# A retention layer and two feed-forward networks on one core: new start address of the right-hand pools, new pacing of the second network's weight preparation

## The chip, the core and the metric

The kernel runs on one NeuronCore of a Trainium2 chip. Times are device microseconds of one execution of the whole program on that core, from its first to its last instruction and the little that lies around them; lower is better. The core's engines have a queue of instructions each: TensorE (PE, with its weight loads as PEld), VectorE (DVE), ScalarE (ACT), GpSimd (POOL) and SyncE (SP), which here issues all data transfers (DMA).

## What is computed

```python
scores = (q @ k.T) / sqrt(64);  ret = scores * Dmat[head]      # retention: Dmat = gamma**(i-j), i >= j
x = (ret @ v)                        # 4 x 8 heads, 576 positions, 64 wide -> x: 2304 x 512
h = x @ w_in                         # first network: 512 -> 2048
x = (max(h, 0) + alpha * min(h, 0)) @ w_out               # 2048 -> 512
y = (sigmoid(x @ w_gate) * (x @ w_val)) @ w_out2          # second network: 512 -> 1536 -> 512
```

Inputs and output are float32 except the weights, which come as float64.

## The kernel before, in words

The 2304 tokens are cut into five blocks of 256, 512, 512, 512 and 512 (blocks 0 to 4). A float32 operand is held as two halves, hi and lo, both of TensorE's fast float32 type, and a product is three matmuls: hi·hi, hi·lo, lo·hi (`products`, L562). The 128x128 operand is loaded as weights, the operand of 512 (in block 0: 256) columns streams past it; the text calls it the moving operand. ScalarE makes hi by a copy and VectorE makes lo by a subtraction (`split`, L183).

**First network.** `ffn1_h(j, f)` (L573) computes one 128-row slice f of h for block j in 12 matmuls into a PSUM tile `h` (two buffers), ScalarE makes max(h,0) and max(-h,0) (L580, L581), VectorE joins them (L582), and `split` makes the pair `g` (L185, L186). `ffn1_y(j, f)` (L604) multiplies g into four accumulators in 12 matmuls. In blocks 2 to 4, h of slice f is followed on TensorE by y of f-2, h of f+1, y of f-1 and h of f+2. The last of these takes the PSUM buffer of h of slice f and can start only when VectorE's split of slice f has read it. Blocks 0 and 1 run woven together, since the weights are still being converted there; between the slices of blocks 1 to 3 lie the pieces of the retention for the next block. The moving operand of h is the tile `x`, that of y is `g`.

**Second network.** For the block pairs (1, 2) and (3, 4) the gate and value products use a 2x2 scheme of seven products instead of eight (`z_step`, L667, six steps t per pair), then `o_phase` multiplies by the output weights. Block 0 is done plainly at the end (`plain_z`). The seven-product scheme needs weight combinations (`prepare_quarters`, L251), which are made during the first network, stored in DRAM (`td`) and fetched again as `tq`. It also needs combinations of the x blocks (`left_factors`, L639: four adds on GpSimd and seven splits), made for the first pair during block 4.

**One job** of `prepare_quarters` takes two raw weight tiles (512 KB each). For each raw tile ScalarE runs two instructions (L208, L209) and VectorE three (L212, L213, L216), which turn float64 into float32; then GpSimd makes four subtractions (L267), and four times ScalarE copies (L276) and VectorE subtracts (L277); five or so transfers write the result. There are twelve such jobs. The generator of a job is advanced by one stage at each `second_step()` (L320), and `second_pace(every)` (L334), called once per slice f from block 2 on, begins a new job at each `every`-th call.

**Who sets the order.** TensorE's instructions stand in the order of the program. Those of the other four engines are placed by a scheduler, which may move an instruction far ahead of where the program has it. `behind("act", "dve")` (L176) holds it back: everything issued inside is placed after the third most recent urgent split (the splits of g, x and the second network's middle tiles). Before the change it is used in `advance()`, for the first network's weights.

**Memory.** SBUF tiles of 4,096 bytes per partition (slots) come from the left side, where each begins 256 bytes past a multiple of 4,096. Three pools begin at the right end instead: `pad`, `xp` (two tiles of 16 KB, the x blocks) and, after the first network, `wide` (eight slots in their place, seven of which hold `tq` of the odd steps t).

Of the kernel before, what the change touches and what calls it, by code (L numbers as in the profile page):

```python
# [10 lines left out]
F32 = mybir.dt.float32  # L11
# [8 lines left out]
P = 128  # L20
# [36 lines left out]
PACE_B, PACE_C = 0.34, 0.5  # L57


PACE_T = (5, 3)  # L60


def chunks():
# [39 lines left out]
def retention_two_ffn(ctx: ExitStack, tc: tile.TileContext, att, cst, alpha, w1, w2, out):  # L103
# [11 lines left out]


    pad = ctx.enter_context(tc.tile_pool(name="pad", bufs=1, side="right"))
    pad_sb = pad.tile([P, 8], F32, tag="pad", name="pad_sb")
    nc.gpsimd.memset(pad_sb, 0.0)
    x_only = ctx.enter_context(ExitStack())  # L120
    xp = x_only.enter_context(tc.tile_pool(name="xp", bufs=2, side="right"))
# [54 lines left out]
    def behind(*engines):  # L176
        stack = ExitStack()
        for e in engines:
            if len(urgent[e]) > AHEAD:
                stack.enter_context(tc.issue_after(urgent[e][-1 - AHEAD].ins))  # L180
        return stack
# [137 lines left out]

    def second_step():  # L320
        for job, g in list(second):
            if next(g, StopIteration) is StopIteration:
                second.remove((job, g))
                ready.add(job)

    def need(*job):
        while job not in ready:
            if not second or asked:
                begin_job()
            second_step()  # L330
# [3 lines left out]
    def second_pace(every):  # L334
        second_step()
        due[0] += 1
        if due[0] >= every:
            due[0] = 0
            begin_job()
        elif due[0] >= every - 2:  # L340
            ask()
# [456 lines left out]
    def plain_z(f, ws):  # L798
        nb = BLOCKS[0]
        ps = []  # L800
        for w, (pool, tag) in zip(ws, ((ps_h, "h"), (ps_a, "ab"[f % 2]))):
            ps.append(pool.tile([P, nb], F32, tag=tag, name=f"z0_{f}"))
            products(ps[-1], [(w[:, k // 2, k % 2], x0[k // 2][:, :, k % 2]) for k in range(KC)])
            free(w)
        t = small.tile([P, nb], F32, tag="t", name=f"sg0_{f}", bufs=1)
        nc.scalar.activation(t, ps[0], AF.Sigmoid)
        nc.vector.tensor_tensor(out=ps[1], in0=t, in1=ps[1], op=ALU.mult)
        g = half_of_slot(f"p0_{f}")
        split(g[:, 0], g[:, 1], ps[1])
        return g  # L810
# [10 lines left out]
    done = [0]  # L821
# [40 lines left out]
    for j in range(1, NBLK):  # L862
# [13 lines left out]
        for f in range(first, NF1):  # L876
# [4 lines left out]
            if j > 1:  # L881
                second_pace(PACE_T[j == NBLK - 1])
            if j == NBLK - 1:
# [22 lines left out]
    def in_z(n, t):  # L906
        def between(point):
            if point == 0:
                while late:
                    ffn1_y(*late.pop(0))  # L910
            if point == 1 and t + 1 < NSTEP:
                load_quarters(t + 1)
            begin_job() if point % 2 else None
            second_step()
        return between
# [31 lines left out]
    for f in range(NF2):  # L947
# [3 lines left out]
        g = plain_z(f, ws.pop(f))  # L951
# [51 lines left out]
```

## Time and profile before

| what | value |
|---|---|
| median of 3 runs (lowest, highest) | 929.73 us (926.93, 930.13) |
| the profiled execution, its own time | 931.73 us |
| its span, first to last instruction | 930.0 us |
| mean granted TensorE clock, share of 2.4 GHz | 0.991 |
| busy: TensorE, its weight loads | 893.7 us, 742.7 us |
| busy: VectorE, ScalarE, GpSimd | 470.1, 406.2, 118.0 us |
| moved to and from HBM | 171.83 MB read, 47.19 MB written |

How to read it: a busy share is the time in which at least one instruction of an engine ran. Matmuls overlap, so that the start of one group to the start of the next tells their rate better than their durations do. "Idle before" a group is time in which the engine had nothing running, and the name behind the arrow is what ended it.

The stages of the span: 0 to 43 us the first retention pieces, 43 to 160 us blocks 0 and 1 woven, 160 to 203 us the rest of block 1, 203 to 302 us block 2, 302 to 413 us block 3, 413 to 508 us block 4, then the second network: 508 to 701 us blocks 1 and 2, 701 to 874 us blocks 3 and 4, 874 to 930 us block 0.

### The profile page before, as it was taken

Reading aid. Unit: us, or ns where it says so; the run is one execution under the profiler, and the core shown is the slowest. Engines: PE = TensorE matmul, PEld = TensorE weight load, DVE = VectorE, ACT = ScalarE, POOL = GpSimd, SP = SyncE. Lnnn points to the kernel's source line nnn. Section 1 sums busy time; section 2 is a strip of 40 time slices with the busy share of each in tenths; the row PEclk is TensorE's granted clock in tenths of the full one; section 3 lists DMA queues with packets and bytes.
Section 4 is the critical chain, followed back from the end, with each engine's and each line's share of the span. In section 5 each row is a group of like instructions: output and inputs, shape, how many; then the busy total and the mean of one; then the engine's idle time right before and its main releaser. Section 6 shows DMA issues by size and latency. Waiting matters only on the chain.

```text
span 930.0 us, 13173 instructions
## 1 busy us (share of the span) xinstructions
PE 893.7 (96%) x4890; PEld 742.7 (80%) x4890; DVE 470.1 (51%) x765; ACT 406.2 (44%) x772; POOL 118.0 (13%) x111
## 2 busy tenths in 40 slices
PE   5689899999999999999989999999999999999998
PEld 5578788778888878888778888888888888888897
DVE  2799996434444656376954464566333332422121
ACT  3488884333343644367645354444323222422111
POOL 5100004221110231032710010002010000000000
PEclk9799999999999999999999999999999999999999
DMA  9435786733366574479597989899746552469940
GB/s 293 167 115 176 259 310 206 281 137 113 125 214 225 193 262 140 173 255 376 214 384 265 373 347 369 310 340 350 274 147 235 186 192 68 164 247 348 405 194 23
DMA packets 74063, 219.89 MB, mean 236 GB/s; under 512 B 12048, under 2 KB 13072, under 8 KB 74000
## 3 DMA queue, kind: packets, MB, share of 16 engines
q1 hardware_dynamic: 74000, 219.05, 65.7%
q8 instruction: 39, 0.64, 0.3%
q14 instruction: 24, 0.20, 0.1%
HBM read 171.83 MB, written 47.19 MB: 236 GB/s over the span
## 4 chain that ended last, share of the span: by engine, by line
PE 68%; DMA 10%; DVE 10%; ACT 5%; issue 3%; SPq 2%; POOL 2%; ACTq 0%; DVEq 0%; POOLq 0%
PE a L566 14%; PE h L566 10%; PE y L566 10%; PE o_y L566 7%; DMA r<-w 5%; PE z L566 4%; PE c L566 4%; PE b L566 4%; PE e L566 4%; PE o_h L566 4%; DVE r L213 2%; PE o L566 2%; PE o_b L566 2%; PE o_a L566 2%; DVE r L216 1%
## 5 line engine op out<-in xcount | busy, mean ns | idle before, releaser
L566 PE MATMUL h<-x,w 128*128 128x512 f32 (+1 forms) x684 | 151.3, 370 | 14.1 <-DVE g L186 12.1
L566 PEld LDWEIGHTS h<-x,w 128*128 128x128 f32 x684 | 115.6, 190 | 40.2 <-DVE g L186 15.1
L566 PE MATMUL a<-xf,tq 128*128 128x512 f32 x576 | 137.7, 391 | 0.0
L566 PEld LDWEIGHTS a<-xf,tq 128*128 128x128 f32 x576 | 108.2, 188 | 23.3
L566 PE MATMUL y<-g,w 128*128 128x512 f32 x492 | 120.7, 394 | 0.0
L566 PEld LDWEIGHTS y<-g,w 128*128 128x128 f32 x492 | 92.3, 189 | 21.6 <-issue 0.9
L582 DVE SCALAR_TENSOR_TENSOR h<-h,na_sb,t 128x512 f32<-128x512 f32 (+1 forms) x80 | 56.1, 702 | 85.0 <-ACT h L581 84.8
L580 ACT ACTIVATE t<-h 128x512 f32<-128x512 f32 (+1 forms) x80 | 44.1, 551 | 81.1 <-PE h L566 80.9
L566 PE MATMUL o_y<-wo,pp 128*128 128x512 f32 x288 | 73.2, 389 | 0.0
L208 ACT ACTIVATE r<-r 128x512 f32<-128x512 f32 x68 | 45.9, 675 | 53.0 <-DMA r<-w 52.7
L566 PE MATMUL h<-x,v 128*128 128x512 f32 x276 | 68.8, 397 | 0.0
L566 PE MATMUL y<-g,v 128*128 128x512 f32 x276 | 67.0, 392 | 0.0
L566 PEld LDWEIGHTS o_y<-wo,pp 128*128 128x128 f32 x288 | 54.1, 188 | 11.3
L186 DVE TENSOR_TENSOR pp<-p,pp 128x512 fp32r<-128x512 f32 x48 | 34.9, 734 | 54.5 <-ACT pp L185 53.4
L185 ACT ACTIVATE g<-h 128x512 fp32r<-128x512 f32 (+1 forms) x80 | 44.2, 552 | 40.7 <-DVE h L582 40.4
L186 DVE TENSOR_TENSOR g<-h,g 128x512 fp32r<-128x512 f32 (+1 forms) x80 | 50.7, 634 | 22.0 <-ACT g L185 18.5
L566 PEld LDWEIGHTS h<-x,v 128*128 128x128 f32 x276 | 51.1, 187 | 12.5 <-issue 0.2
L566 PEld LDWEIGHTS y<-g,v 128*128 128x128 f32 x276 | 51.5, 188 | 11.8 <-issue 0.5
L267 POOL TENSOR_TENSOR r<-r,r 128x256 f32<-128x256 f32 x24 | 24.7, 1027 | 284.7 <-DVE r L216 284.7
L185 ACT ACTIVATE pp<-p 128x512 fp32r<-128x512 f32 x48 | 30.0, 630 | 60.5 <-PE o_h L566 32.2
L213 DVE CUSTOM_DVE_ANT_0 r<-r,top 128x1024 uint16<-128x1024 uint16 x68 | 48.1, 712 | 3.6 <-ACT r L209 1.0
L216 DVE SCALAR_TENSOR_TENSOR r<-r 128x512 uint32<-128x512 uint32 x68 | 47.3, 699 | 0.5
(102 smaller groups left out, 1293.2 us busy)
## 6 DMA issues: line engine op xcount, KB each, us to landing
tq<-td SPq DMA_DIRECT2D x84, 512.0 KB, 5.0
r<-w SPq DMA_DIRECT2D x68, 512.0 KB, 5.2
wo<-wod SPq DMA_DIRECT2D x60, 512.0 KB, 5.8
v<-w1d SPq DMA_DIRECT2D x46, 512.0 KB, 5.0
td<-q SPq DMA_DIRECT2D x36, 512.0 KB, 4.5
zp<-td SPq DMA_DIRECT2D x48, 256.0 KB, 5.7
kv<-att SPq DMA_DIRECT2D x16, 512.0 KB, 4.5
qk<-att SPq DMA_DIRECT2D x15, 512.0 KB, 4.7
```

What stands on the lines that cost most here:

```text
L185: a = nc.scalar.activation(hi, src, AF.Copy)
L186: d = nc.vector.tensor_tensor(out=lo, in0=src, in1=hi.bitcast(F32), op=ALU.subtract)
L208: nc.scalar.activation(high.bitcast(F32), high.bitcast(F32), AF.Copy, scale=2.0 ** -112)
L213: nc.vector.tensor_tensor(out=low.bitcast(I32), in0=low.bitcast(I32), in1=top.bitcast(I32), op=ALU.add)
L216: nc.vector.scalar_tensor_tensor(low, high, 0x80000000, low, ALU.bitwise_and, ALU.bitwise_or)
L267: sub = lambda o, a, b: nc.gpsimd.tensor_tensor(out=o, in0=a, in1=b, op=ALU.subtract)
L566: nc.tensor.matmul(ps, l, r, start=first and i == 0, stop=last and i == len(todo) - 1, skip_group_check=joins)
L580: nc.scalar.activation(t, ps, AF.Relu)
L582: nc.vector.scalar_tensor_tensor(ps, ps, na_sb[:, f:f + 1], t, ALU.mult, ALU.add)
```

## The change

```diff
-PACE_T = (5, 3)
+PACE_T = (4, 4)
...
     pad = ctx.enter_context(tc.tile_pool(name="pad", bufs=1, side="right"))
-    pad_sb = pad.tile([P, 8], F32, tag="pad", name="pad_sb")
+    pad_sb = pad.tile([P, 184], F32, tag="pad", name="pad_sb")
...
     def second_step():
         for job, g in list(second):
-            if next(g, StopIteration) is StopIteration:
+            with behind("act", "dve"):
+                done = next(g, StopIteration) is StopIteration
+            if done:
                 second.remove((job, g))
                 ready.add(job)
```

The pad grows from 32 to 736 bytes, so that the right-hand tiles move down by 704 bytes: they begin at 1,984 modulo 2,048 before and at 1,280 modulo 2,048 after (960 and 256 modulo 1,024); the left ones stay at 256 modulo 2,048. The first number of `PACE_T` holds in blocks 2 and 3, the second in block 4: a job began at each fifth, then each third slice, and now at each fourth throughout. And the stages of the jobs are held behind the urgent splits.

TensorE's instructions keep their order. Four engines' queues change. In the rows below `r2_...` is a raw tile of a job, `top` its scratch, `q` one of its results, `xf` a split left factor, `x2` a block of x fetched for it, `t`, `h` and `g` the slice tiles of the first network (block, then slice); the numbers behind are the program's own.

VectorE in the woven blocks 0 and 1, before:

```order
L186 TENSOR_TENSOR g0_12_1453<-h0_13_1526,g0_12_1453 128x256
L216 SCALAR_TENSOR_TENSOR r2_0_1_2476<-r2_0_1_2476 128x512
L212 TENSOR_SCALAR top_2727<-r2_6_1_2478 128x512
L582 SCALAR_TENSOR_TENSOR h1_9_1549<-h1_9_1549,na_sb_90,t1_9_1562 128x512
L213 ISA r2_6_1_2478<-r2_6_1_2478,top_2727 128x512x2
L216 SCALAR_TENSOR_TENSOR r2_6_1_2478<-r2_6_1_2478 128x512
L186 TENSOR_TENSOR g1_9_1566<-h1_9_1549,g1_9_1566 128x512
L212 TENSOR_SCALAR top_2965<-r2_1_0_2771 128x512
L213 ISA r2_1_0_2771<-r2_1_0_2771,top_2965 128x512x2
L216 SCALAR_TENSOR_TENSOR r2_1_0_2771<-r2_1_0_2771 128x512
L582 SCALAR_TENSOR_TENSOR h0_14_1593<-h0_14_1593,na_sb_90,t0_14_1606 128x256
L186 TENSOR_TENSOR g0_14_1610<-h0_14_1593,g0_14_1610 128x256
```

and now:

```order
L186 TENSOR_TENSOR g0_12_1453<-h0_13_1526,g0_12_1453 128x256
L584 SCALAR_TENSOR_TENSOR h1_9_1549<-h1_9_1549,na_sb_90,t1_9_1562 128x512
L186 TENSOR_TENSOR g1_9_1566<-h1_9_1549,g1_9_1566 128x512
L584 SCALAR_TENSOR_TENSOR h0_14_1593<-h0_14_1593,na_sb_90,t0_14_1606 128x256
L186 TENSOR_TENSOR g0_14_1610<-h0_14_1593,g0_14_1610 128x256
```

Five raw tiles of the second network were converted there; they now stand in block 2, two raw tiles of a job next to each other.

VectorE in block 4, from the split of slice 6 to that of slice 7, before (the first eleven of twelve instructions between them) and now (seven between them):

```order
L186 TENSOR_TENSOR g4_6_4105<-h4_6_4088,g4_6_4105 128x512
L186 TENSOR_TENSOR xf0_7_1_4350<-s0_1_1_4330,xf0_7_1_4350 128x512
L277 TENSOR_TENSOR q4_0_0_4319<-r2_4_0_4066,q4_0_0_4319 128x4x128
L186 TENSOR_TENSOR xf0_5_1_4338<-s0_1_0_4329,xf0_5_1_4338 128x512
L277 TENSOR_TENSOR q4_0_2_4394<-r2_10_0_4068,q4_0_2_4394 128x4x128
L212 TENSOR_SCALAR top_4559<-r2_5_0_4408 128x512
L213 ISA r2_5_0_4408<-r2_5_0_4408,top_4559 128x512x2
L216 SCALAR_TENSOR_TENSOR r2_5_0_4408<-r2_5_0_4408 128x512
L582 SCALAR_TENSOR_TENSOR h4_7_4127<-h4_7_4127,na_sb_90,t4_7_4140 128x512
L277 TENSOR_TENSOR q4_0_1_4322<-r2_4_0_4066,q4_0_1_4322 128x4x128
L186 TENSOR_TENSOR xf0_3_1_4353<-s0_1_1_4330,xf0_3_1_4353 128x512
L186 TENSOR_TENSOR xf0_6_1_4341<-s0_1_0_4329,xf0_6_1_4341 128x512
```

```order
L186 TENSOR_TENSOR g4_6_4145<-h4_6_4128,g4_6_4145 128x512
L277 TENSOR_TENSOR q4_0_2_4251<-r2_10_0_3929,q4_0_2_4251 128x4x128
L277 TENSOR_TENSOR q4_0_3_4254<-r2_10_0_3929,q4_0_3_4254 128x4x128
L186 TENSOR_TENSOR xf0_5_1_4365<-s0_1_0_4356,xf0_5_1_4365 128x512
L584 SCALAR_TENSOR_TENSOR h4_7_4164<-h4_7_4164,na_sb_90,t4_7_4177 128x512
L186 TENSOR_TENSOR xf0_6_1_4368<-s0_1_0_4356,xf0_6_1_4368 128x512
L186 TENSOR_TENSOR xf0_4_1_4374<-x2_0_3_4264,xf0_4_1_4374 128x512
L186 TENSOR_TENSOR xf0_7_1_4377<-s0_1_1_4357,xf0_7_1_4377 128x512
L186 TENSOR_TENSOR g4_7_4181<-h4_7_4164,g4_7_4181 128x512
```

A raw tile's conversion (L212, L213, L216) and half of the splits of left factors have left this place; in all of block 4 VectorE has one instruction less.

SyncE in block 4, the loads of the first left factors, before and now:

```order
L200 DMA r2_4_1_4232<-w2 128x1024
L637 DMA x2_0_1_4236<-x2d1_165 128x512
L637 DMA x2_0_1_4236<-x2d2_166 128x512
L291 DMA td3_7_147<-q3_1_3_4221 128x512
L292 DMA td3_6_146<-q3_1_3_4221 128x512
L637 DMA x2_0_2_4073<-x2d1_165 128x512
L637 DMA x2_0_2_4073<-x2d2_166 128x512
```

```order
L291 DMA td3_7_147<-q3_0_3_3877 128x512
L292 DMA td3_6_146<-q3_0_3_3877 128x512
L200 DMA r2_4_1_4106<-w2 128x1024
L639 DMA x2_0_2_4113<-x2d1_165 128x512
L639 DMA x2_0_2_4113<-x2d2_166 128x512
L639 DMA x2_0_0_4110<-x2d1_165 128x512
L639 DMA x2_0_0_4110<-x2d2_166 128x512
```

The second half of the first factors' input, `x2_0_2`, was fetched behind the stores of job (3, 1)'s last result; it now stands behind those of job (3, 0), ahead of the stores that end block 3.

ScalarE in block 4, now, the last eleven of the fourteen instructions between the copies of slices 2 and 3, and the copy of slice 3; before, five stood between them:

```order
L209 ACTIVATE r2_4_0_3927<-r2_4_0_3927 128x512
L208 ACTIVATE r2_10_0_3929<-r2_10_0_3929 128x512
L209 ACTIVATE r2_10_0_3929<-r2_10_0_3929 128x512
L185 ACTIVATE xf0_1_0_4196<-x2_0_0_4110 128x512
L185 ACTIVATE xf0_5_0_4199<-s0_0_0_4190 128x512
L582 ACTIVATE t4_3_4006<-h4_3_3993 128x512
L583 ACTIVATE h4_3_3993<-h4_3_3993 128x512
L185 ACTIVATE xf0_6_0_4202<-s0_0_0_4190 128x512
L185 ACTIVATE xf0_3_0_4214<-s0_0_1_4191 128x512
L185 ACTIVATE xf0_2_0_4205<-x2_0_2_4113 128x512
L185 ACTIVATE xf0_4_0_4208<-x2_0_2_4113 128x512
L185 ACTIVATE g4_3_4010<-h4_3_3993 128x512
```

Six copies of left factors that were spread over slices 3 to 5 now stand in slice 3.

## Rows read from the trace of the kernel before

**Rows 1.** The page, part 1: busy time and its share of the span.

```profile
PE 893.7 (96%) x4890; PEld 742.7 (80%) x4890; DVE 470.1 (51%) x765; ACT 406.2 (44%) x772; POOL 118.0 (13%) x111
```

**Rows 2.** Busy time by stretch: PE, PEld, DVE, ACT, POOL, then clock, DMA share, GB/s.

```profile
43.00:160.00 117.00, 107.59 (x669) 94.15 (x666) 104.33 (x194) 90.18 (x184) 10.77 (x10) 0.99 0.62 216
...
440.00:474.00 34.00, 29.65 (x121) 23.36 (x120) 29.71 (x41) 22.89 (x42) 18.32 (x11) 0.95 0.72 260
...
508.00:625.00 117.00, 117.00 (x516) 96.47 (x515) 63.25 (x103) 52.75 (x90) 4.28 (x4) 1.00 0.93 347
...
468.00:474.00 6.00, 6.00 (x20) 4.75 (x21) 4.00 (x7) 4.03 (x8) 0.00 (x0) 0.72 0.99 352
```

**Rows 3.** Timeline of TensorE, 440 to 480 us: start, duration, group, count, [idle before].

```profile
452.98 3.06 PE L566 MATMUL h<-x,w 128*128 128x512 f32 x12 [0.82 <-DVE g L186]
...
458.64 2.96 PE L566 MATMUL h<-x,w 128*128 128x512 f32 x12
...
467.87 4.35 PE L566 MATMUL h<-x,w 128*128 128x512 f32 x12 [3.53 <-DVE g L186]
472.02 3.21 PE L566 MATMUL y<-g,w 128*128 128x512 f32 x12
```

**Rows 4.** The chain of waits that ended in that idle time: start, duration, what.

```profile
436.80 6.37 DMA x<-x2d
...
443.23 4.30 POOL s L643
...
465.41 1.80 DVE xf L186 x3
```

**Rows 5.** Timeline of TensorE at the end of the first network, 500 to 512 us.

```profile
502.77 2.96 PE L566 MATMUL h<-x,v 128*128 128x512 f32 x12
505.57 2.90 PE L566 MATMUL y<-g,v 128*128 128x512 f32 x12
508.31 2.88 PE L566 MATMUL a<-xf,tq 128*128 128x512 f32 x12
511.03 5.60 PE L566 MATMUL y<-g,v 128*128 128x512 f32 x24
```

**Rows 6.** Timeline of TensorE, odd steps t of the second network, both pairs.

```profile
535.54 2.91 PE L566 MATMUL e<-xf,tq 128*128 128x512 f32 x12
538.28 2.91 PE L566 MATMUL a<-xf,tq 128*128 128x512 f32 x12
...
726.73 2.96 PE L566 MATMUL c<-xf,tq 128*128 128x512 f32 x12
729.52 2.73 PE L566 MATMUL a<-xf,tq 128*128 128x512 f32 x11
```

**Rows 7.** Timeline of TensorE, groups of 256 columns, blocks 0 of both networks.

```profile
149.18 1.54 PE L566 MATMUL h<-x,w 128*128 128x256 f32 x12
...
874.71 5.92 PE L566 MATMUL z<-x,zp 128*128 128x256 f32 x48
```

**Rows 8.** Timeline of TensorE, two more waits for a split, blocks 1 and 3.

```profile
151.45 3.07 PE L566 MATMUL h<-x,w 128*128 128x512 f32 x12 [0.73 <-DVE g L186]
...
341.75 3.06 PE L566 MATMUL h<-x,w 128*128 128x512 f32 x12 [0.17 <-DVE g L186]
```

**Rows 9.** Instructions by line and shape: count, busy us, mean ns of one, idle before.

```profile
L582 DVE SCALAR_TENSOR_TENSOR h<-h,na_sb,t 128x512 f32<-128x512 f32 x64 | 48.4, 756 | 84.8 <-ACT h L581 84.8
L213 DVE CUSTOM_DVE_ANT_0 r<-r,top 128x1024 uint16<-128x1024 uint16 x68 | 48.1, 712 | 3.6 <-ACT r L209 1.0
...
L186 DVE TENSOR_TENSOR g<-h,g 128x512 fp32r<-128x512 f32 x64 | 44.0, 688 | 19.9 <-ACT g L185 16.4 <-DMA r<-w 2.7
...
L277 DVE TENSOR_TENSOR q<-r,q 128x512 fp32r<-128x512 f32 x48 | 38.6, 813 | 10.4 <-ACT q L276 9.9 <-issue 0.2
...
L186 DVE TENSOR_TENSOR xf<-s,xf 128x512 fp32r<-128x512 f32 x16 | 16.4, 1033 | 7.8 <-ACT xf L185 7.2
...
L208 ACT ACTIVATE r<-r 128x512 f32<-128x512 f32 x68 | 45.9, 675 | 53.0 <-DMA r<-w 52.7
...
L580 ACT ACTIVATE t<-h 128x512 f32<-128x512 f32 x64 | 38.0, 594 | 79.5 <-PE h L566 79.3
```

## The prediction, as it was made

> **What bounds the kernel now.** First the busy times: TensorE is busy for 893.7 of 930.0 us, VectorE and ScalarE for half [rows 1]. So only two things can shorten the span: matmuls that run at a higher rate, and TensorE's idle time. The busy times by stretch show where the idle time lies. From 508 us on TensorE has none; from 43 to 160 us it lacks 9.4 us while VectorE is busy for 104.3 of 117; in block 4, from 440 to 474 us, it lacks 4.35 us, and the granted clock falls to 0.72 at its end [rows 2]. The timeline of TensorE shows these two holes: a slice's h waits 0.82 us and a later one 3.53 us for the split g of a slice two before; the second hole is followed by groups of 4.35 and 3.21 us, where others take 2.96 and 2.90 [rows 3, 5]. The chain of waits tells why: a fetch of x blocks that takes 6.37 us, GpSimd's adds behind it (4.30 us for one), then VectorE's splits of left factors, with g queued behind three of them [rows 4].
>
> Everywhere else the rate of matmuls decides, and it is not the same everywhere. From start to start, twelve matmuls of h take 2.80 us (505.57 - 502.77), twelve of y 2.74, and twelve of the second network's first product 2.72 [rows 5]. All have 512 columns; h streams `x`, which lies in a right-hand pool, y and the product stream left-hand tiles.
>
> **The change, part by part.**
>
> *1. Start address, moving operand.* Each h of 512 columns may fall from 2.80 to y's 2.74, or to 2.72 [rows 5]. I take 2.74, since y is its neighbour in the same stage. There are 64 such groups, 16 slices in four blocks, but the first eleven of block 1 lie in the woven stretch, where TensorE waits for VectorE anyway. That leaves 53 x 0.06 = 3.2 us. Bounds: nothing, and 53 x 0.08 = 4.2.
>
> In the woven stretch block 0's groups have 256 columns, and there the address may cost: h from the right takes (1.54 - 0.28)/11 = 0.115 us per matmul, and z, whose operands lie on the left, (5.92 - 0.28)/47 = 0.120, with 0.28 as an estimate of the last matmul's own duration, a little over twice the 0.12 between starts [rows 7]. Sixteen groups of twelve lose 16 x 12 x 0.0055 = 1.1 us against 11 x 0.06 = 0.7 gained by block 1's. VectorE's queue covers either; I count nothing, with bounds of -0.7 and +1.1. If that cover went, the +0.4 would show.
>
> *2. Start address, weights.* In the odd steps t of the second network `tq` lies on the right: a group takes 2.74 (538.28 - 535.54), against 2.72 in the first, even step [rows 5, 6]. Six such steps of seven groups of twelve, 42 x 0.02 = 0.8; and one `xf` tile on the right makes group c 2.79 instead of 2.74, six times: 0.3 [rows 6]. Together 1.1 us, bounds 0 and 1.6.
>
> That such an address matters at all is what the rows show: 2.80 beside 2.72 for twelve groups of the same shape at the same clock [rows 2, 5]. The Trainium skill, "TensorE: Matmul & The Clock Gate", section "Wait — 56ns, not 53.3ns?", has one number for a matmul at full clock, its columns over 2.4 GHz and 2.5 ns, 216 ns at 512 columns, with no term for an address. By it both address terms would be nothing; no group here runs at that figure, 2.72 us being 227 ns each. That reading is the first rival.
>
> *3. Block 4.* The two holes cost 0.82 + 3.53, the two groups behind the longer one 1.39 + 0.31 (4.35 - 2.96, 3.21 - 2.90), as the clock stood at the 1.2 GHz level for part of that stretch after the idle time, and the group behind the shorter one 0.10: 6.15 us [rows 2, 3, 5]. The new order takes away what the chain is made of. SyncE fetches the first factors' input before the end of block 3's stores, so that GpSimd can add early; and between the splits of slices 6 and 7 VectorE has seven instructions, six of them not the slice's own, instead of twelve. A split's own path is 0.59 + 0.59 + 0.76 + 0.59 + 0.69 = 3.2 us [rows 9], and from the end of h to the h two later there are y, h and y, 2.74 + 2.80 + 2.74 = 8.3 [rows 5]: 5.1 us of slack. Six others of 0.69 to 1.03 [rows 9] are 4.1 to 6.2, and part of them runs while ScalarE works on the slice. So the hole closes, just.
>
> *4. Smaller waits.* One wait in block 3, 0.17 us and 0.10 of a longer group, and one in the woven blocks, 0.73 and 0.11 [rows 5, 8]. Before the latter VectorE converted raw tiles of the second network, which have left that place: 1.1 us in all. The rest of the woven stretch's waits stand behind the first network's own weights and stay.
>
> *5. What is put in.* No instruction is added; twelve jobs stay twelve. In blocks 2 and 3 a job's two tiles now stand together: six instructions of at most 0.71 us, 4.3 at most [rows 9], inside the 5.1 of slack. The tightest place is ScalarE in block 4 between the copies of slices 2 and 3: fourteen instructions at 0.59 to 0.68 [rows 9], 8.3 to 9.5 us, then copy and split, 1.28. From slice 2's copy (2.5 us after its h) there are 5.5 + 8.3 - 2.5 = 11.3 us. Between 0.5 and 1.7 are left, with every input on time. One split of left factors there, or a conversion that GpSimd slows, may come 1 us late. I count +1.0 for new waits; bounds 0, and 5.2 for a hole like the old one with its slow clock (3.53 + 1.39 + 0.31). SyncE's queue holds the same transfers; the fetches of first-network weights stand behind results that VectorE makes at least one slice earlier, and no wait of TensorE for them shows before. Their cover is that slice of 5.5 us.
>
> *Sum:* -3.2 - 1.1 - 6.15 - 1.1 + 1.0 = -10.55 us. The profiled execution took 931.73, so 921.2; the median of the runs is 2.0 lower than that execution, so **919.2, say 919**.
>
> **The rivals.**
>
> *The address gives nothing.* The new start is 1,280 modulo 2,048, not the left side's 256, so that only half of what distinguishes the sides is removed; no 512-column group of before streams from there. Against it: z's operands at both places of 256 columns run alike. Then -6.15 - 1.1 + 1.0 = -6.25: 923.5.
>
> *The block-4 wait moves to slice 3.* ScalarE's fourteen in a row there leave 0.5 us or so; if GpSimd's first adds come late as in the chain of before [rows 4], a hole of the old size returns: 5.2 in place of 1.0, 919.2 + 4.2 = 923.4.
>
> *Slower: the paired conversions stall blocks 2 to 4.* VectorE's split with a GpSimd-made input takes 1.03 us where g takes 0.69 [rows 9], 1.5 times. If GpSimd's subtractions of one job run under the next pair, 4.3 becomes 6.4, over the slack of 5.1, and each such place makes a hole with slow clock of 5.2. It decides from three of the eight or so pairs on (919.2 + 3 x 5.2 = 934.8); I take four, 940.0. The Trainium skill, "SBUF — State Buffer", section "Who interferes with whom", states that VectorE with two SBUF inputs contends with GpSimd's reads; the 1.03 agrees. Against it: jobs begin four slices, some 22 us, apart, so a pair seldom meets subtractions.
>
> **How the numbers follow.** Forecast 0.70, no gain by address 0.13, wait moved to slice 3 0.12, slower 0.05. The runs of before scatter from 926.93 to 930.13. About 0.5% (4.65 us) is what a measurement can tell from no change: faster is under 925.1, slower over 934.4. The forecast counts as faster but for 0.02, the next two for four fifths: 0.68 + 0.10 + 0.09 = 0.87, of which I give 0.01 to no change; slower is the last case. Low end: 4.2 and 1.6 for the addresses, 0.7 in the woven stretch and no new wait, 931.7 - 13.75 - 2.0 = 916.0, less 1.5 of scatter: 914.5. High end: the two middle rivals at 923.5 with 2 of scatter: 925.5.
>
> **What would show it.** Step 1: twelve h from start to start 2.74 or less in blocks 2 to 4. Step 2: odd steps like even ones. Step 3: no idle time over 0.5 us and clock 1.00 from 440 to 474 us. Step 4: no wait near 151 and 341 us. Step 5: holes, if any, at h of slices 5 or 6 of block 4, or two slices behind a pair in blocks 2 and 3. Wrong would be: h still at 2.80, or a hole over 3 us with a fallen clock behind it.

## The result and the profile after

The changed kernel took 918.67 us (median of four runs, 917.01 to 919.67) beside 929.93 us for the kernel before on the same chip (926.93 to 931.36): ratio 0.9881, 95% interval 0.9852 to 0.9911. Timed a second time, in the experiments below, it took 916.60 beside 929.62: 0.9854 (0.9836 to 0.9872). The forecast was 919.0, its range 914.5 to 925.5.

The profiled execution took 917.86 us, its span is 916.0. First the page, part 1, of the changed kernel, for the row of [rows 1]:

```profile
PE 882.7 (96%) x4890; PEld 741.3 (81%) x4890; DVE 465.6 (51%) x765; ACT 404.9 (44%) x772; POOL 109.9 (12%) x111
```

TensorE runs the same 4,890 matmuls and is busy for 11 us less. Part of that is time at the lower clock that is gone, and part is matmuls that got shorter: with the new order alone TensorE is busy for 888.1 us, with the new address alone for 885.1 (e5 and e1 below). Busy time by stretch, columns as in [rows 2] (the stretches are cut at the times of before, though the changed kernel runs ahead of it):

```profile
43.00:160.00 117.00, 106.49 (x655) 94.08 (x655) 92.63 (x174) 83.43 (x171) 2.34 (x2) 0.99 0.63 213
...
203.00:302.00 99.00, 99.00 (x622) 81.26 (x621) 50.39 (x83) 45.43 (x89) 19.45 (x21) 1.00 0.52 183
302.00:413.00 111.00, 111.00 (x632) 91.57 (x631) 63.39 (x103) 53.68 (x99) 20.12 (x23) 1.00 0.68 235
...
440.00:474.00 34.00, 34.00 (x152) 28.15 (x151) 25.23 (x35) 22.17 (x42) 13.17 (x12) 1.00 0.91 328
```

Three things are to be seen. From 203 to 474 us TensorE has no idle time left, and in block 4 it runs 152 matmuls in the 34 us in which it ran 121 [rows 2], at the full clock. VectorE and GpSimd are relieved between 43 and 160 us (92.6 us against 104.3, 2.3 against 10.8), since the second network's conversions have left. And TensorE gained nothing there: its idle time is 10.5 us, 9.4 before.

The rate of the matmuls, first in block 4, then in the odd steps of the second network (timeline of TensorE: start, duration, group, count):

```profile
479.52 2.88 PE L568 MATMUL h<-x,v 128*128 128x512 f32 x12
482.24 2.88 PE L568 MATMUL y<-g,v 128*128 128x512 f32 x12
484.96 2.88 PE L568 MATMUL h<-x,v 128*128 128x512 f32 x12
...
523.43 2.88 PE L568 MATMUL e<-xf,tq 128*128 128x512 f32 x12
526.15 2.88 PE L568 MATMUL a<-xf,tq 128*128 128x512 f32 x12
...
534.31 2.88 PE L568 MATMUL c<-xf,tq 128*128 128x512 f32 x12
537.03 5.60 PE L568 MATMUL a<-xf,tq 128*128 128x512 f32 x24
```

Twelve h take 482.24 - 479.52 = 2.72 us, 0.08 less than before [rows 5], and y also takes 2.72, 0.02 less. In the odd steps e and c take 2.72, where 2.74 and 2.79 stood [rows 6]. A slice of h and y is 5.44 us instead of 5.54.

Groups of 256 columns go the other way, as [rows 7] let fear (changed kernel, timeline of TensorE in the woven blocks):

```profile
145.51 1.60 PE L568 MATMUL h<-x,w 128*128 128x256 f32 x12
146.95 0.88 PE L568 MATMUL y0a<-g,w 128*128 128x256 f32 x6
```

Block 0's h took 1.54 us for twelve and takes 1.60; from start to start it is 1.44, 0.120 a matmul.

To compare stages whose starts have moved I read, in the timelines of TensorE, when the first matmul of a stage begins. The table gives the time between such starts (the last row ends where TensorE's last matmul ends) in the profiled executions of before, of the changed kernel twice (the second is run c256 below), and of two experiments that come next.

| from, to | before | changed | again | e1: pad | e5: order |
|---|---|---|---|---|---|
| start of the span to block 0's first h | 43.1 | 39.9 | 41.3 | 40.1 | 39.4 |
| to block 2's first h (woven stretch, end of block 1) | 159.7 | 162.7 | 160.1 | 162.2 | 160.5 |
| to block 4's first h (blocks 2 and 3) | 210.4 | 206.2 | 206.7 | 206.8 | 209.2 |
| to the second network (block 4) | 95.1 | 87.0 | 87.1 | 92.9 | 88.7 |
| to the end of TensorE's last matmul | 417.6 | 416.2 | 416.1 | 415.8 | 417.1 |

The first row is chance: the order there is untouched, and in twelve profiles of kernels that have it in common it takes from 38.8 to 43.1, that of before being the longest. So the two spans (930.0 and 916.0) differ by 3.2 us more than the change explains. Without that row before takes 882.8 us, the changed kernel 872.1 and 870.0: 10.7 and 12.8 us less.

### The profile page after: what moved, and what is told of

Same layout as the page of the kernel before. It is cut to its first block, busy times and chain, and to the rows that moved or that the text cites. A ratio compares the mean times of both kernels' runs of the same rounds, so it can differ in the third digit from the quotient of the medians.

```text
span 916.0 us, 13165 instructions
## 1 busy us (share of the span) xinstructions
PE 882.7 (96%) x4890; PEld 741.3 (81%) x4890; DVE 465.6 (51%) x765; ACT 404.9 (44%) x772; POOL 109.9 (12%) x111
## 4 chain that ended last, share of the span: by engine, by line
PE 85%; DVE 5%; ACT 4%; DMA 3%; issue 1%; SPq 1%; POOL 0%; ACTq 0%; DVEq 0%; POOLq 0%
PE h L568 18%; PE y L568 17%; PE a L568 14%; PE o_y L568 7%; PE z L568 4%; PE o_h L568 4%; PE c L568 4%; PE b L568 4%; PE e L568 4%; PE o L568 2%; PE o_b L568 2%; PE o_a L568 2%; PE s L457 1%; PE o L496 1%; PE o L476 1%
## 5 line engine op out<-in xcount | busy, mean ns | idle before, releaser
L568 PE MATMUL h<-x,w 128*128 128x512 f32 (+1 forms) x684 | 146.9, 365 | 10.5 <-DVE g L186 9.1
L568 PEld LDWEIGHTS h<-x,w 128*128 128x128 f32 x684 | 116.2, 190 | 32.3 <-DVE g L186 10.5
L216 DVE SCALAR_TENSOR_TENSOR r<-r 128x512 uint32<-128x512 uint32 x68 | 47.4, 710 | 0.2
L213 DVE CUSTOM_DVE_ANT_0 r<-r,top 128x1024 uint16<-128x1024 uint16 x68 | 45.7, 688 | 1.1
L209 ACT ACTIVATE r<-r 128x512 int32<-128x512 uint32 x68 | 45.5, 669 | 0.0
```

Of the source, the lines that this page charges most:

```text
L209: nc.scalar.activation(low.bitcast(I32), low, AF.Copy, scale=2.0 ** -29)
L213: nc.vector.tensor_tensor(out=low.bitcast(I32), in0=low.bitcast(I32), in1=top.bitcast(I32), op=ALU.add)
L216: nc.vector.scalar_tensor_tensor(low, high, 0x80000000, low, ALU.bitwise_and, ALU.bitwise_or)
L568: nc.tensor.matmul(ps, l, r, start=first and i == 0, stop=last and i == len(todo) - 1, skip_group_check=joins)
```

## The experiments

**Address and order apart.** e1 is the kernel before with the new pad alone, so that every engine's instructions stand as before; e5 has the new order with the old addresses (VectorE's instructions stand in exactly the order of the changed kernel). e1, e5, e2 and e3 are timed beside the same runs of the kernel before.

```diff
e1_pad, on the kernel before:
-    pad_sb = pad.tile([P, 8], F32, tag="pad", name="pad_sb")
+    pad_sb = pad.tile([P, 184], F32, tag="pad", name="pad_sb")
e5_order, on the changed kernel:
-    pad_sb = pad.tile([P, 184], F32, tag="pad", name="pad_sb")
+    pad_sb = pad.tile([P, 8], F32, tag="pad", name="pad_sb")
```

> Only the pad grows (184 words); every engine's instructions stand as in the kernel before. Theory (the start address sets the rate): terms 1 and 2 of the forecast, -3.2 - 1.1 = -4.3 us, ratio 0.9954; from the trace of the changed kernel rather more, -6 to -8 (0.992 to 0.9935), since its y and z groups seem shorter too. Twelve h from start to start 2.72 to 2.74 us in block 4, the two holes of block 4 still there. Rival (address gives nothing, all comes from the order): 929.9 us, ratio 1.000, h still 2.80.

> Only the order of the jobs changes (PACE_T (4, 4) and second_step behind the urgent splits); the pad stays at 8 words, all addresses are the old ones. Theory: terms 3 to 5 of the forecast, -6.15 - 1.1 + 1.0 = -6.25 us, ratio 0.9933; if the woven stretch gives nothing back, rather -4 to -5 (0.995). h stays 2.80, no idle time over 0.5 us from 440 to 474 us. Rival (address and order lean on each other, the shorter matmuls need the new order or the reverse): e1 and e5 together come to clearly less or more than the 11.3 us of the whole change, by 2 us or more.

Measured: e1 923.34 us, ratio 0.9938 (0.9917 to 0.9959); e5 921.74 us, ratio 0.9906 (0.9889 to 0.9923); the kernel before 930.28. e1's timeline of TensorE in block 4, with the rate of the changed kernel and a hole of the old kind:

```profile
441.84 2.88 PE L566 MATMUL h<-x,w 128*128 128x512 f32 x12
444.56 2.88 PE L566 MATMUL y<-g,w 128*128 128x512 f32 x12
450.74 4.50 PE L566 MATMUL h<-x,w 128*128 128x512 f32 x12 [3.29 <-DVE g L186]
455.07 2.88 PE L566 MATMUL y<-g,w 128*128 128x512 f32 x12
...
463.79 3.02 PE L566 MATMUL h<-x,w 128*128 128x512 f32 x12 [0.40 <-DVE g L186]
```

And e5's, with the old rate (2.80, 2.74) and no hole:

```profile
453.45 2.96 PE L568 MATMUL h<-x,w 128*128 128x512 f32 x12
456.25 2.90 PE L568 MATMUL y<-g,w 128*128 128x512 f32 x12
458.99 2.96 PE L568 MATMUL h<-x,w 128*128 128x512 f32 x12
```

What follows: the two parts act by different means, the address on the rate of the matmuls and the order on the holes, and each does by itself what it does in the whole change. "Address gives nothing" falls: e1's interval ends at 0.9959, and its instructions differ in nothing but where the right-hand tiles lie. In the table the address alone (e1 against before) gives 3.6 us in blocks 2 and 3 and 1.8 in the second network; on top of the order (changed against e5) 3.0, 1.7 in block 4 and 0.9. The order alone (e5 against before) gives 6.4 us in block 4 and 1.2 in blocks 2 and 3. By the medians e5 gains 8.5 us, more than the 6.25 that were expected at most; without the start-up row of the table it is 7.3, with 1.2 in blocks 2 and 3 and 0.5 in the second network. Do the two lean on each other? Their gains by the ratios, 0.62% and 0.94%, make 1.56%, or 14.5 us; the whole change gave 1.19% (11.1 us) and, again, 1.46% (13.6 us). The rival asked for 2 us or more: against the first it is 3.4, against the second 0.9. Without the start-up row of the table they give 5.1 + 7.3 = 12.4 against 10.7 and 12.8. So they add up within intervals of some 2 us to either side for each; an interplay of 2 us or a little more is not excluded.

**The order's two parts.** e2 is the kernel before with the stages held behind the splits and the old pace; e3 has the new pace alone.

```diff
e2_behind, on the kernel before:
-            if next(g, StopIteration) is StopIteration:
+            with behind("act", "dve"):
+                done = next(g, StopIteration) is StopIteration
+            if done:
e3_pace, on the kernel before:
-PACE_T = (5, 3)
+PACE_T = (4, 4)
```

> Only second_step is held behind the urgent splits; PACE_T stays (5, 3), pad 8 words. VectorE then converts no raw tile of the second network in blocks 0 and 1, but ten in block 4 (before: five and six), with 15 instructions between the splits of slices 3 and 4 and 12 between those of slices 6 and 7. Theory A (what counts is how many instructions stand between two splits in block 4): the holes of block 4 stay or grow, 929 to 935 us, ratio 0.999 to 1.006. Theory B (what counts is that urgent splits go first): holes gone, -5 to -6.2, ratio 0.9935 to 0.995.

> Only PACE_T becomes (4, 4); second_step is not held behind the splits, pad 8 words. Between the splits of slices 4 and 5 stand 4 VectorE instructions (11 before), between those of slices 6 and 7 four (3 of the jobs' own kind and less; 12 before); the five conversions in the woven stretch stay. Theory A (crowding in block 4 made the holes, the pace spreads it): holes gone, -5 to -6.2 us, ratio 0.9935 to 0.995; the wait near 151 us stays. Theory B (only holding the jobs behind the splits removes them): 928.5 to 930.5, ratio 0.9985 to 1.0005, holes still there or moved.

Measured: e2 930.84 us, ratio 1.0005 (0.9989 to 1.0021); e3 923.60 us, ratio 0.9932 (0.9906 to 0.9959). Theory A holds in both (e3's 6.7 us are a little over the 5 to 6.2 expected). The busy time from 440 to 474 us, of e2:

```profile
440.00:474.00 34.00, 29.34 (x116) 23.41 (x115) 27.55 (x40) 20.79 (x38) 14.82 (x12) 0.90 0.74 250
```

and of e3:

```profile
440.00:474.00 34.00, 34.00 (x148) 27.47 (x148) 20.44 (x29) 18.58 (x34) 9.74 (x8) 1.00 0.73 245
```

In e2 one longer hole, at slice 6's h, has taken the place of the two at slices 7 and 9; in e3 a short wait is left, at slice 4's h. e2's timeline of TensorE:

```profile
446.59 5.49 PE L568 MATMUL h<-x,w 128*128 128x512 f32 x12 [4.66 <-DVE g L186]
451.88 3.29 PE L568 MATMUL y<-g,w 128*128 128x512 f32 x12
```

and e3's:

```profile
432.53 3.06 PE L566 MATMUL h<-x,w 128*128 128x512 f32 x12 [0.74 <-DVE g L186]
435.42 2.93 PE L566 MATMUL y<-g,w 128*128 128x512 f32 x12
```

The crowd decides: how many VectorE instructions stand between the splits of two neighbouring slices of block 4 was 11 and 12 at its worst before, 15 and 12 in e2, 9 in e3 and in the changed kernel. Block 4 as a whole is no emptier: VectorE converts six raw tiles in it before, eight in the changed kernel. Holding the stages back moves jobs later, out of the woven blocks and with the old pace into block 4, where e2 converts ten. Together with the pace it seems to help: in the one profile of each, e5 is 1.0 us ahead of e3 in block 4 (88.7 against 89.7), which is the wait at slice 4 and the somewhat longer groups behind it, and five of e3's splits end less than 0.8 us before the h that needs them, none of e5's less than 0.9. By their times the two can't be told apart (0.9906 and 0.9932, with intervals that overlap).

One rival is left: the new pace also brings the first factors' input early. The first four of its eight loads are issued 11.9 to 20.0 us after block 4's first h before the change, but from 1.1 us ahead of that h to 0.9 us after it in e3, and from 0.4 ahead to 8.7 after in the changed kernel. Early loads do not close the hole by themselves: in n_ahead3 below they are issued from 0.9 ahead to 9.6 after, 12 instructions stand between the splits of slices 2 and 3, and a wait of 4.01 us follows.

A second rival, GpSimd, can be read from the traces. VectorE and GpSimd before the change, between the splits of slices 6 and 7 (timelines: start, duration, instruction):

```profile
458.25 1.74 POOL L643 TENSOR_TENSOR s<-s,x 128x512 f32<-128x512 f32 x1
458.76 1.79 DVE L186 TENSOR_TENSOR xf<-s,xf 128x512 fp32r<-128x512 f32 x1
...
465.33 1.28 DVE L186 TENSOR_TENSOR xf<-s,xf 128x512 fp32r<-128x512 f32 x2
```

A split of this kind takes 1.79 us while GpSimd adds, and about 0.68 when GpSimd is idle. In all fourteen profiles VectorE's subtractions with both inputs in SBUF (those that make `xf`, `q` and `w`) take 0.70 us at most when no GpSimd instruction runs beside them and up to 1.8 when one does; the 512-column split of g, which reads one input from PSUM, never takes over 0.70. Between the splits of slices 6 and 7 this costs VectorE some 3.0 us before and 3.2 in the changed kernel. So it makes a crowd longer than its number says, but it is not what the change took away.

**Which property of the address.** Four pads on the changed kernel (below in the order a832, a896, a768, a512) separate multiples of 64, 128 and 256 bytes from the left side's own place, 256 modulo 1,024. The starts are those of the program's allocation; no trace shows an address.

```diff
-    pad_sb = pad.tile([P, 184], F32, tag="pad", name="pad_sb")
+    pad_sb = pad.tile([P, 40], F32, tag="pad", name="pad_sb")
...
+    pad_sb = pad.tile([P, 24], F32, tag="pad", name="pad_sb")
...
+    pad_sb = pad.tile([P, 56], F32, tag="pad", name="pad_sb")
...
+    pad_sb = pad.tile([P, 120], F32, tag="pad", name="pad_sb")
```

> The changed kernel with a pad of 40 words: the right-hand tiles begin at 832 modulo 1,024, a multiple of 64 bytes as the 960 of before, but 128 bytes lower. Theory A (a start that is a multiple of 128 bytes or more is what helps): as slow as 960, twelve h of 512 columns 2.80 us, six slices of block 4 33.2 us (e5: 33.2; the changed kernel: 32.6). Theory B (only the place 256 modulo 1,024 helps, so that both operands begin alike): the same here.

> The changed kernel with a pad of 24 words: right-hand tiles at 896 modulo 1,024, a multiple of 128 bytes and not of 256. Theory A (128 suffices): h 2.72 to 2.74 us, six slices 32.6. Theory A2 (256 is needed) and theory B (only 256 modulo 1,024): h 2.80, six slices 33.2.

> The changed kernel with a pad of 56 words: right-hand tiles at 768 modulo 1,024, a multiple of 256 bytes, 512 away from the left tiles' 256. Theory A and A2 (a multiple of 128 or 256 suffices): h 2.72 to 2.74, six slices 32.6. Theory B (only 256 modulo 1,024): 2.80 and 33.2, or a value between.

> The changed kernel with a pad of 120 words: right-hand tiles at 512 modulo 1,024. Theory A and A2: h 2.72 to 2.74, six slices 32.6; if larger multiples help more, h under 2.72. Theory B (only 256 modulo 1,024): 2.80 and 33.2. The groups of 256 columns of block 0, 0.115 us a matmul at 960 and 0.120 at 256 modulo 1,024, say whether these go with h or against it.

Measured, a single time of each, so that only the rates are compared: a832 926.61 us, a896 923.89, a768 916.27, a512 913.96. The neighbouring groups h and y in block 4, timeline of TensorE, first a832:

```profile
479.04 2.93 PE L568 MATMUL h<-x,v 128*128 128x512 f32 x12
481.81 2.93 PE L568 MATMUL y<-g,v 128*128 128x512 f32 x12
484.58 2.93 PE L568 MATMUL h<-x,v 128*128 128x512 f32 x12
```

then a896:

```profile
482.45 2.96 PE L568 MATMUL h<-x,v 128*128 128x512 f32 x12
485.24 2.90 PE L568 MATMUL y<-g,v 128*128 128x512 f32 x12
487.97 2.96 PE L568 MATMUL h<-x,v 128*128 128x512 f32 x12
```

then a768 and a512:

```profile
483.39 2.88 PE L568 MATMUL h<-x,v 128*128 128x512 f32 x12
486.11 2.88 PE L568 MATMUL y<-g,v 128*128 128x512 f32 x12
488.83 2.88 PE L568 MATMUL h<-x,v 128*128 128x512 f32 x12
```

```profile
481.12 2.88 PE L568 MATMUL h<-x,v 128*128 128x512 f32 x12
483.84 2.88 PE L568 MATMUL y<-g,v 128*128 128x512 f32 x12
486.56 2.88 PE L568 MATMUL h<-x,v 128*128 128x512 f32 x12
```

| right-hand start modulo 1,024 | largest power of two that divides it | h, us | y, us | second network to the end, us |
|---|---|---|---|---|
| 960 (e5) | 64 | 2.80 | 2.74 | 417.1 |
| 832 (a832) | 64 | 2.77 | 2.77 | 419.5 |
| 896 (a896) | 128 | 2.79 | 2.73 | 419.0 |
| 768 (a768) | 256 | 2.72 | 2.72 | 416.1 |
| 512 (a512) | 512 | 2.72 | 2.72 | 416.1 |
| 256 (changed) | 256 | 2.72 | 2.72 | 416.2 |

A2 stands: of the six starts the three that are multiples of 256 bytes run alike, those that are multiples of 64 or 128 alone don't. Why it is 256 stays open. That both operands begin at the same place (theory B) is not what counts. And the groups on either side are not independent: y, whose operands lie on the left, is 0.01 to 0.05 slower wherever h's are off. In e5's last slices of block 4 all twelve matmuls of an h follow each other after 233 or 234 ns, those of the y behind it after 226 to 235 for the first five and after 226 to 228 from then on. The Trainium skill, "TensorE: Matmul & The Clock Gate", section "Wait — 56ns, not 53.3ns?", gives 216 ns for 512 columns at full clock; the best here, 2.72 / 12 = 227, stays above it. By that figure alone an address would cost nothing. The rows decide: 0.08 / 12 = 7 ns a matmul lie between the starts 960 and 256.

**Is there a better place, and what bounds the woven stretch?** n512 is a512 again, timed beside the changed kernel itself (c256). The other two change AHEAD, the number of urgent splits by which weight stages may run ahead, on top of a512.

```diff
n_ahead1, on a512:
-AHEAD = 2
+AHEAD = 1
n_ahead3, on a512:
-AHEAD = 2
+AHEAD = 3
```

> The kernel of a512 again, timed: the change with the right-hand tiles at 512 instead of 256 modulo 1,024. Its one time was 913.96 us. Theory (any multiple of 256 bytes gives the same rate; the single time owes its advantage to a start-up 0.8 us shorter, a woven stretch without a fall of the clock and a 1.7 us shorter wait near 192 us, none of which hangs on the address): within its interval of the changed kernel, 917 to 919.5 us. Rival (512 is better than 256): 913.5 to 915, clear of the changed kernel in the same call.

> The changed kernel itself, timed beside n512 on the same chip. Theory: 918.7 as before, within half a microsecond or so of n512; its profile shows other waits near 126 and 192 us than the first one if those come from chance. Rival: 4 us above n512.

> The change with 512 modulo 1,024 and AHEAD = 1: the weights' stages stand behind the last but one urgent split instead of the last but two. Theory A (in the woven stretch the splits wait behind weight stages on VectorE's queue): TensorE's waits for g from 43 to 160 us, 9.1 us in 6 in the changed kernel, fall by 2 us or more, 914 to 917 us. Theory B (the raw tiles' round of load, ScalarE and VectorE sets the pace there): holding the stages back longer delays the weights by as much, 918 to 924 us.

> As n_ahead1 with AHEAD = 3: the weights' stages may go one split earlier. Theory A: more instructions ahead of the splits, the waits for g grow by 1 to 4 us, 919 to 923 us. Theory B (the raw tiles' round sets the pace, and stages that go earlier free raw tiles earlier): waits fall, 914 to 917 us.

Measured, beside 929.62 us for the kernel before: n512 918.99 us, ratio 0.9871 (0.9851 to 0.9890); c256 916.60, 0.9854 (0.9836 to 0.9872); n_ahead1 922.13, 0.9917 (0.9899 to 0.9935); n_ahead3 930.01, 1.0002 (0.9991 to 1.0013). So a512's single 913.96 was chance, and no version here beats the change. c256 came out 2.4 us below n512, where half a microsecond was expected, and 2.1 below its own first median; the intervals of c256 and n512 overlap. TensorE's waits for g from 43 to 160 us (total us, times, longest), in n_ahead1 and n_ahead3:

```profile
PE h L568 <- DVE g L186: 10.5, 5, 3.5
```

```profile
PE h L568 <- DVE g L186: 12.3, 6, 3.1
```

The changed kernel has 9.1 and 7.8 us of these waits in its two profiles. AHEAD = 3 does what theory A says, and more: a hole of 4.01 us comes back in block 4, at slice 5, with longer matmuls behind it, and one of 1.86 at slice 9 (n_ahead3, timeline of TensorE):

```profile
440.98 4.61 PE L568 MATMUL h<-x,w 128*128 128x512 f32 x12 [4.01 <-DVE g L186]
445.43 2.91 PE L568 MATMUL y<-g,w 128*128 128x512 f32 x12
```

AHEAD = 1 does what theory B says. Most of what AHEAD = 3 loses lies not in the woven stretch but in block 4, 95.1 us against n512's 87.0, since the second network's jobs are held back less, too. For the woven stretch this leaves open which theory holds: 162.6 us there with AHEAD = 3 is inside what the twelve profiles with AHEAD = 2 show (158.7 to 163.2), 165.8 with AHEAD = 1 is outside. By the time of the whole program 2 lies between two worse values.

## Why the prediction was right

The time, 918.67 and 916.60, lies at 919.0 and a little below. That it is so close is in part luck, since two errors of some microseconds stood against each other (see the sum). Step by step:

**1. Moving operand.** The mechanism was right, the size too small. I took y's 2.74 as the rate h would reach; the runs show 2.72, and y itself falls from 2.74 to 2.72. A slice thus gains 0.10 us, not 0.06: 53 x 0.10 = 5.3 instead of 3.2, and outside the bound of 4.2, which left out that the neighbour gains too. The step that failed is "I take 2.74, since y is its neighbour in the same stage": the neighbour was slowed by the same cause. The worry in the first rival, that 1,280 modulo 2,048 is only half of what distinguishes the sides, is settled by a768 and a512.

The 256-column groups came out as worked out, 0.120 instead of 0.115 a matmul. Whether they cost anything can't be seen: block 0's first h to block 2's takes 159.7, 160.5, 159.3, 160.1, 162.5 and 163.2 us in the six profiles with a start that is no multiple of 256 bytes and AHEAD = 2 (before, e5, e2, e3, a832, a896), and 162.2, 162.7, 160.1, 159.3, 158.7 and 159.6 in the six with such a start (e1, changed, c256, a768, a512, n512). Their means are 160.9 and 160.4.

**2. Weights on the right.** 1.1 us was forecast; the second network takes 1.4 and 1.5 less, and odd steps run like even ones.

**3. Block 4.** 6.15 us was forecast; e5, which has the order alone, gains 6.4. No wait over 0.5 us is left from 440 to 474, and the clock is 1.00. The forecast gave the credit to both edits, the loads that come early and the shorter queue. e2 and e3 show that the pace carries most of it (5.4 of the 6.4 us), and that holding the stages back without it is worth nothing (1.0005). The rows of the order need a correction: between the splits of slices 6 and 7 five splits of left factors stood before and four stand now, so that one has left, not half of them. And the instructions there were priced too low: 1.03 us is a mean of 0.68 alone and up to 1.79 beside GpSimd, so that the six others took 7.3 us by their durations in the changed kernel, over the 6.2 that I gave as the most and over the slack of 5.1. No wait came of it: the split of slice 7 still ended 1.8 us before slice 9's h began.

**4. Smaller waits.** Block 3's wait of 0.17 us is gone, and so is one of 0.50 at block 2's first h in the first profile of the changed kernel, which I had not counted (in c256 it stands at 0.23, so part of it is chance). The wait at 151 us is gone too, but its 0.84 us is not gained. The reason that I gave, VectorE's conversions in front of the split, held for that wait and not for the stretch. VectorE has 11.7 us less to do there, and other waits stand or grow elsewhere, now at 124.71 and 128.58 us. The changed kernel's timeline of TensorE:

```profile
113.53 3.01 PE L568 MATMUL h<-x,w 128*128 128x512 f32 x12 [2.33 <-DVE g L186]
...
124.71 1.70 PE L568 MATMUL h<-x,w 128*128 128x256 f32 x12 [1.14 <-DVE g L186]
128.58 4.61 PE L568 MATMUL h<-x,w 128*128 128x512 f32 x12 [2.17 <-DVE g L186]
```

What is late instead? VectorE itself now waits in that stretch for ScalarE, 11.3 us in eight waits, where before it was 3.5 in three (VectorE's waits from 43 to 160 us, changed kernel: total us, times, longest):

```profile
DVE h L584 <- ACT h L583: 11.3, 8, 3.0
DVE g L186 <- ACT g L185: 5.5, 9, 0.9
```

and SyncE's queue holds the loads of raw weights until VectorE's last step frees a tile (waits of SyncE's queue there):

```profile
SPq L200 <- DVE w L227: 39.5, 15, 5.2
```

Before, that wait of the loads was 41.2 us in 16, hardly more. The chain of waits that ends at 128.58 us in the changed kernel runs through such a round of a raw tile (VectorE frees it, load, ScalarE, VectorE):

```profile
116.56 0.69 DVE w L227
...
117.65 6.08 DMA r<-w
...
125.77 0.61 DVE r L213
...
128.10 0.44 DVE g L186
```

The runs show that less work for VectorE buys nothing there: without those five conversions e2 and e5 take 159.3 and 160.5 us to block 2's first h, the kernel before 159.7. That the round of five raw tiles is the bound is read from these waits and not shown: a sixth tile was not tried.

**5. New waits.** I counted 1.0 us; in blocks 2 to 4 there are none. The rivals "slower" and "moved to slice 3" had no trace in the changed kernel: blocks 2 and 3 are busy throughout, and slice 3, with ScalarE's fourteen in a row, makes no wait: its split ends 0.7 us before slice 5's h begins, 1.1 in c256, inside the 0.5 to 1.7 that were forecast.

**Sum.** By the table, without the start-up row: -4.2 and -3.7 in blocks 2 and 3 (forecast -1.9 for 32 slices and -0.27), -8.1 and -8.0 in block 4 (-6.15 and -0.96 for 16), -1.4 and -1.5 in the second network (-1.1), +3.0 and +0.4 in the woven stretch and the end of block 1 (-1.1). That is -10.7 and -12.8 against -10.55: an address term too small by some 2 us, and 1.0 us of waits that did not come, stood against a woven stretch that gave nothing back. The terms of blocks 2 to 4 and of the second network come to -13.7 and -13.2 against -10.4 without the new waits, so the sum came out closer than its terms. Of the +3.0 in the first profile 1.5 is one wait near 192 us that is 1.74 there, 0.53 in c256 and 0.29 before, with no instruction or transfer named as its end (changed kernel, timeline of TensorE):

```profile
194.21 1.16 PE L457 MATMUL s<-qk 64*128 64x128 f32 x16 [1.74 <-issue]
```

The setting of the sum, 2.0 us below the profiled execution, was right, and the table gives a likely reason that I did not know: that execution had the longest start of all the profiles.

## What to carry to other kernels

Compare the start-to-start time of equal groups of matmuls between stages: where one stage is 3% slower at the same clock and without idle time, look at the addresses of its operands, and try a pool at a multiple of 256 bytes; here it took a pad of a few hundred bytes and was worth as much as the stage was slower, times every such group, and some more in the groups beside it. This held for 512 columns; groups of 256 became slower. Where TensorE waits for splits, count what stands between two splits on the queue in that block before changing priorities: spreading jobs evenly over blocks gave most of it here, while holding them back alone only pushed the crowd into a later block. And look at what GpSimd runs beside them, since a split of left factors took 0.68 us or up to 1.79. Before an engine is relieved, ask what it waits for itself: in the woven stretch 11.7 us less work for VectorE made nothing shorter.

## What the runs showed of the hardware that was not expected

- The start of a right-hand tile changes the rate of 512-column matmuls: 2.72 us for twelve at the multiples of 256 bytes tried, 2.77 at 832, 2.79 and 2.80 at 896 and 960 modulo 1,024. The groups beside it take their share, most at 832 (y 2.77), so that h and y together take 5.52 to 5.54 us at all three and 5.44 at the multiples of 256. The second network loses more at 832 and 896 (419.5 and 419.0 us against 416.2) than at 960 (417.1).
- For 256 columns the same step goes the other way: 0.115 us a matmul at 960 [rows 7], 0.120 at 256 modulo 1,024. The other starts follow the same line: 0.118 at 832, 0.119 at 896, 0.120 at 768 and 512. Why is open.
- VectorE's subtractions with both inputs in SBUF take about 0.68 us alone and up to 1.8 beside GpSimd; with one input in PSUM they stay at 0.70 or less in either case (fourteen profiles).
- A wait's length did not tell whether the clock falls: after 2.33 us of idle time twelve h took 3.01 us, after 2.17 us, 15 us later and with a wait of 1.14 ahead of it, 4.61, with seven matmuls about 427 ns apart. The granted clock is 1.00 from 112 to 120 us and 0.72 from 128 to 134, so that part of the latter ran at the 1.2 GHz level. The Trainium skill, "TensorE: Matmul & The Clock Gate", section "Wait — 56ns, not 53.3ns?", gives 426.7 ns for 512 columns at that level, and the trace agrees.
- The time until block 0's first h differs by 4.3 us (38.8 to 43.1) between profiles of kernels that have the same instructions there, which is more than most parts of this change are worth. Two profiles should be compared from a common event on.
